# Second weights of the first two experts issued by GpSimd behind the row gathers, with new gather costs in the planner

## Chip, cores and metric

The kernel runs on one core of one Trainium2 chip, in one launch. The metric is the device time of one execution in microseconds. The runs are compared by their medians, and one further execution was profiled.

## What is computed

The reference has three parts in a row, all in float32 (the weights of the middle part come as float64):

- an mLSTM attention over 4 batches, 8 heads, 768 positions and a head dimension of 40, with gates; its output is laid out as 3072 tokens of 320 numbers;
- a feed-forward layer 320 -> 2048 -> 320 with a clipped quadratic activation;
- a mixture of 8 experts. Each token goes to one expert, greedily by the logits of a gate, with at most 384 tokens for an expert:

```python
cap = N // E
for idx in np.argsort(-logits.flatten()):
    tok, e = int(idx) // E, int(idx) % E
    if assigned[tok] >= 0 or counts[e] >= cap: continue
    assigned[tok] = e; counts[e] += 1
for e in range(E):
    h = np.maximum(x[assigned == e] @ w1[e], 0.0)
    out[assigned == e] = h @ w2[e]
```

An expert has 384 tokens, w1 of 320 x 1024 and w2 of 1024 x 320.

## The kernel before, in words

**The stages.** Attention (24 chunks of 128 tokens) runs beside the feed-forward layer (8 groups of 384 tokens, 16 slices of 128 hidden units each) until some 570 us. The result of the feed-forward layer, x2, is written to DRAM (`x2_d`, line 880) 128 rows at a time. Then the experts follow, counted here as the code does, from `ph` = 0 to 7, and called expert 0 to expert 7.

**An expert.** `route(ph)` finds which expert is filled next, and which tokens go to it, by a search over six groups of bits of the logits. Each of its six steps is a short chain VectorE mask `m` (L1039), TensorE count `pc` (L1098), VectorE `ev`, TensorE `ps` (L1112), VectorE `ok`, TensorE `pj` (L1122), VectorE `y`. It yields the expert's number `ei` and, through `slots()`, the indices `idx` of its 384 tokens. `gather(ph, idx)` has GpSimd issue three indirect DMAs (L1253), each of which fetches 128 rows of 1280 bytes out of `x2_d` into `xg`; ScalarE copies a part of the tile (L1257), TensorE transposes it into `pxe` (L639), and `split_x` splits that into a rounded part `xh_e` (ScalarE L641) and a rest `xl_e` (VectorE L645; L647 writes the rest of the last 64 rows into `xh_e`). `weights(ph, ei)` has SyncE read the number of the expert into a register (L1269) and issue the loads: four pieces of w1, each of one DMA of 262 KB and two of 65 KB (L1281, L1284), and four pieces of w2, each of one DMA of 328 KB (L1294, two blocks of 128 rows of 1280 bytes). Each piece is split by ScalarE and VectorE (w1: L1287, L1289; w2: L1296, L1298). The raw pieces have three buffers for each kind, so the fourth piece is loaded when the first is split. `expert()` then runs, for each of eight slices of 128 hidden units, eight matmuls up into `pf` (L788), a ReLU and a split (L1320, L1321), and nine matmuls down into `pe` (L854), two slices behind. At its end the three results are copied into `os` (L1336) and GpSimd scatters them into the output (L1339). `prepare(ph + 1)` (gather and weights of the next expert) is listed inside `expert(ph)` at its ninth turn, and route steps of later experts are put between its matmuls. Until the first gather lands, TensorE is given empty matmuls on a constant (`pdm`, L349).

**What sets the order.** Nothing above is issued where it stands in the source. `add()` makes a step with an engine, an estimated duration `dur`, for a DMA its transfer time `dma`, and a latency `lat`, and with the steps that it needs: by the tiles that it reads and writes, and by the list `after`. `order()` is a list scheduler. It plans all steps by these numbers, and `issue()` then emits them in the planned order of start, so that each engine's instructions have a fixed order. `after` and the costs are known to the planner alone. At run time an engine takes its instructions in that order, and an instruction waits only for the data that it reads and the buffers that it overwrites. For a DMA the planner reckons

```python
if s.dma:
    if e == "S":
        hw = max(hw, end) + 0.45
        dma = max(dma, hw + 0.65) + s.dma
    else:
        dma = max(dma, end + 1.55) + s.dma
    end = dma + 0.9
```

and whatever needs it is ready `lat` (HOP = 0.17 where not given) later. A gather has `dur` 1.05 and `dma` 0.46, so that an undisturbed one lands 1.05 + 1.55 + 0.46 + 0.9 + 0.17 = 4.13 us after its start in the plan, and the third of three 6.23 us after the start of the first.

Of the kernel before, what the change touches and what calls it, by code (L numbers as in the profile page):

```python
# [19 lines left out]
P = 128  # L20
L = 128
TG = 384
HOP = 0.17
# [21 lines left out]
class Plan:  # L45
# [12 lines left out]
    def add(self, eng, dur, fn, r=(), w=(), after=(), dma=0.0, lat=HOP, pre=0, act=1.0, due=None, flat=False):  # L58
        s = Step()
        s.flat = flat  # L60
        s.act, s.due, s.crit, s.mark = act, due, self.crit, self.mark
        s.eng, s.dur, s.lat, s.fn, s.dma = eng, dur, lat, fn, dma
        s.need, s.ready, s.users, s.seq, s.start = 0, 0.0, [], len(self.steps) - pre, None
        s.tiles = []
        deps = set(after)
        for key in r:
            deps.update(self.wr.get(key, ()))
        for key in w:
            deps.update(self.wr.get(key, ()))
            deps.update(self.rd.get(key, ()))  # L70
        for key in r:
            self.rd.setdefault(key, []).append(s)
        for key in w:
            self.wr[key] = [s]
            self.rd[key] = []
        for key in list(r) + list(w):
            t = key[0] if isinstance(key, tuple) else key
            if isinstance(t, Slot) and t not in s.tiles:
                s.tiles.append(t)
                t.left += 1  # L80
        for d in deps:
            d.users.append(s)
            s.need += 1
        self.steps.append(s)
        return s
# [151 lines left out]
def cost_act(n, ap=False, psum=True):  # L237
    return (0.095 if psum else 0.137) + n * 0.00072 + (0.093 if ap else 0.0)


def cost_v(n, fast=False):
    return 0.069 + n * (0.00052 if fast else 0.00104)
# [7 lines left out]
def kernel(  # L250
# [17 lines left out]
    V, A, G, T, S = nc.vector, nc.scalar, nc.gpsimd, nc.tensor, nc.sync  # L268
# [7 lines left out]
    NE = w_gate.shape[1]  # L276
    NC = NTOK // P
# [29 lines left out]
    add = pl.add  # L307

    def at(pool):
        return lambda: pool  # L310
# [10 lines left out]
    def dma(fn, n, r=(), w=(), rate=360.0, after=(), pre=0, dur=0.05, due=None):  # L321
        return add("S", dur, fn, r, w, dma=n / (rate * 1e3), after=after, pre=pre, due=due)
# [43 lines left out]
    x2_d = pl.tile(at(dram), [NTOK, DM], F32, "x2_d", 1)  # L366
# [4 lines left out]
    def c2(t):  # L371
# [6 lines left out]
        r=[gf, gi], w=[gm])  # L378
# [10 lines left out]
        r=[fz, gm], w=[gf])  # L389
# [3 lines left out]
    def t_it():  # L393
# [4 lines left out]
        r=[ps_it], w=[it])  # L398
# [232 lines left out]
    def split_x(x, xh, xl, t, ps, pre=0, due=None):  # L631
        cs = slice(t * P, (t + 1) * P)

        def px():
            return ps()[:, :3 * P].rearrange("p (j l) -> p j l", j=3)

        def t_x():
            for j in range(3):
                T.transpose(px()[:, j, :], x()[:, j * P:(j + 1) * P], ident())  # L639
        add("T", 0.33, t_x, r=[x, identr], w=[ps], due=due)  # L640
        add("A", cost_act(384), lambda: A.activation(xh()[:, :, cs], px(), AF.Copy), r=[ps], w=[(xh, t)])  # L641

        def hf():
            return xh().bitcast(F32)
        add("V", cost_v(256), lambda: V.tensor_tensor(xl()[:, :, cs], px()[:, :2, :], hf()[:, :2, cs], op=OP.subtract),  # L645
            r=[ps, (xh, t)], w=[(xl, t)], pre=pre)
        add("V", cost_v(128), lambda: V.tensor_tensor(xh()[KR:, 2, cs], px()[KR:, 2, :], hf()[KR:, 2, cs], op=OP.subtract),  # L647
            r=[ps], w=[(xh, t)], pre=pre)
# [27 lines left out]
    def piece(name):  # L676
        return pl.tile(at(wpool), [P, 2, 3, 2 * P], F32R, "w1", 8, name)
# [210 lines left out]
    def pd(shape, dtype, name, bufs=1, tag=None):  # L888
        return pl.tile(later("pd"), shape, dtype, tag or name, bufs, name)
# [120 lines left out]
    def psd(tag, name, bufs=1):  # L1010
        return pl.tile(later("psd"), [P, 512], F32, tag, bufs, name)
# [235 lines left out]


    def gather(ph, idx):
        xg = []  # L1250
        for t in range(GC):
            x = pd([P, 3 * P], F32, f"xg{ph}_{t}", 3, "xg")
            add("G", 1.05, lambda t=t, x=x: G.indirect_dma_start(  # L1253
                out=x()[:, :DM], out_offset=None, in_=x2_d(),
                in_offset=bass.IndirectOffsetOnAxis(ap=idx()[:, t:t + 1], axis=0)),
                r=[idx] + [(x2_d, n) for n in range(NC)], w=[x], dma=0.46)
            add("A", cost_act(KR, psum=False), lambda x=x: A.activation(x()[:, DM:], x()[:, 2 * P:DM], AF.Copy), w=[x])  # L1257
            xg.append(x)
        xh = pl.tile(at(p2), [P, 3, TG], F32R, "xh", 2, f"xh_e{ph}")
        xl = pl.tile(at(p2), [P, 2, TG], F32R, "xl", 2, f"xl_e{ph}")  # L1260
        for t in range(GC):
            split_x(xg[t], xh, xl, t, psd("psf", f"pxe{ph}_{t}", 3), 100000)
        return xh, xl

    def weights(ph, ei):
        w1t = [piece(f"w1t{ph}_{i}") for i in range(F2 // (2 * P))]
        w2t = pl.tile(at(wpool), [P, 2, NF2, DM], F32R, "w2", 2, f"w2t{ph}")
        ev = []
        add("S", 1.1, lambda: ev.append(S.value_load(ei()[0:1, 0:1], min_val=0, max_val=NE - 1)), r=[ei], w=[(ei, "reg")])  # L1269
        ek = [(ei, "reg")]  # L1270

        def w1e():
            return w1[bass.ds(ev[0], 1)].rearrange("o d f -> (o d) f")

        def w2e():
            return w2[bass.ds(ev[0], 1)].rearrange("o f d -> (o f) d")
        for s in range(4):
            cs = slice(s * 256, (s + 1) * 256)
            r1 = pd([P, 3, 256], F32, f"r1_{ph}_{s}", 3, "r1")
            hold = late_x[:0] if ph == 0 and s >= 2 else []  # L1280
            dma(lambda cs=cs, r1=r1: S.dma_start(r1()[:, :2, :], w1e()[:2 * P, cs].rearrange("(k p) f -> p k f", p=P)),  # L1281
                262e3, r=ek, w=[(r1, 0)], dur=0.55, after=hold)
            for i in range(2):
                dma(lambda cs=cs, r1=r1, i=i: S.dma_start(r1()[i * KR:(i + 1) * KR, 2, :], w1e()[2 * P:, cs]),  # L1284
                    65e3, r=ek, w=[(r1, 1 + i)], dur=0.55, after=hold)
            rk = [(r1, i) for i in range(3)]
            add("A", cost_act(768, psum=False), lambda s=s, r1=r1: A.activation(w1t[s]()[:, 0], r1(), AF.Copy),  # L1287
                r=rk, w=[(w1t[s], 0)])
            add("V", cost_v(768), lambda s=s, r1=r1: V.tensor_tensor(  # L1289
                w1t[s]()[:, 1], r1(), w1t[s]().bitcast(F32)[:, 0], op=OP.subtract), r=rk + [(w1t[s], 0)], w=[(w1t[s], 1)])  # L1290
        for s in range(4):
            fs = slice(s * 2, (s + 1) * 2)
            r2 = pd([P, 2, DM], F32, f"r2_{ph}_{s}", 3, "r2")
            dma(lambda s=s, r2=r2: S.dma_start(r2(), w2e()[s * 2 * P:(s + 1) * 2 * P, :].rearrange("(k p) d -> p k d", p=P)),  # L1294
                328e3, r=ek, w=[r2], dur=0.55, after=hold)
            add("A", cost_act(640, psum=False), lambda fs=fs, r2=r2: A.activation(w2t()[:, 0, fs, :], r2(), AF.Copy),  # L1296
                r=[r2], w=[(w2t, 0, s)])
            add("V", cost_v(640), lambda fs=fs, r2=r2: V.tensor_tensor(  # L1298
                w2t()[:, 1, fs, :], r2(), w2t().bitcast(F32)[:, 0, fs, :], op=OP.subtract), r=[r2, (w2t, 0, s)], w=[(w2t, 1, s)])
        return w1t, w2t  # L1300
# [47 lines left out]

    def prepare(ph):
        ei, idx = plan[ph]  # L1350
        return (idx, *gather(ph, idx), *weights(ph, ei))

    plan, pend = [], None
    for ph in range(NE):
        pl.crit = ph == 0
        ei, slots = route(ph)
# [12 lines left out]
    if 1:  # L1369
        pdm2 = psd("psf", "pdm2", 3)  # L1370
        add("T", 0.22, filler(pdm2)(2), r=[quart, NEXT], w=[pdm2])
    ready = prepare(0)
    if 1:
        stop = next(st for st in pl.steps if st.eng == "T" and any(x.name == f"pxe0_{0}" for x in st.tiles))
# [44 lines left out]
```

## Time and profile before

| | us |
|---|---|
| runs | 851.94, 852.33, 848.98 (median 851.94) |
| the profiled execution, own time | 848.75 |
| its span in the profile | 847.0 |
| around the span | 1.75 |
| TensorE busy (94% of the span) | 800.3 |
| VectorE busy (74%) | 626.9 |
| ScalarE busy (55%) | 463.9 |
| GpSimd busy (26%) | 221.8 |

The times of the rows below are microseconds from the start of the span. PE is TensorE's matmuls, PEld its weight loads, DVE VectorE, ACT ScalarE, POOL GpSimd, SP SyncE. Instructions that only issue a DMA do not count as busy on SP; the indirect DMAs on POOL do. PEclk is the granted TensorE clock, 1.00 for 2.4 GHz and 0.50 for 1.2 GHz. Where a row groups instructions of one line, it gives the shortest, median and longest in ns; the rows on the tile xg give the time from a gather's issue to its landing. An engine that is idle costs nothing unless what follows on it is late for the end.

### The profile page before, as it was taken

The page shows a single profiled execution, that of the slowest core. Times are in us where ns is not written, and L with a number is a line of the kernel's source. Part 1 is how long each engine was busy: PE and PEld are TensorE (multiplying, and loading weights), DVE is VectorE, ACT ScalarE, POOL GpSimd, SP SyncE. Part 2 cuts the span into 40 slices and gives each one's busy share as a digit, 9 for nine tenths or more (in the row PEclk, how much of TensorE's full clock was granted, in tenths as well). Part 3 has the DMA queues.
Part 4 walks back from the last instruction along what each step waited for, and adds up shares of the span by engine and source line. Part 5 has one row for each costly group of instructions (what it writes and reads, how often), then busy time and mean ns, then how long its engine had stood idle before and what let it go on. Part 6 is the DMA issues. An engine that isn't in the chain of part 4 may idle for free. (4 is left out here: it accounts for less than half of the span.)

```text
span 847.0 us, 15577 instructions
## 1 busy us (share of the span) xinstructions
PE 800.3 (94%) x5493; PEld 748.6 (88%) x5493; DVE 626.9 (74%) x1534; ACT 463.9 (55%) x1002; POOL 221.8 (26%) x315
## 2 busy tenths in 40 slices
PE   8998999999999999999999999997979699999896
PEld 7886889999999999999999998897959598898896
DVE  7888887587877787787887667656768687897561
ACT  4476868666566566566666658803232343543451
POOL 4553555121311310211122143002030321321411
PEclk9999999999999999999999999998969699999998
DMA  9897542231431431532321000005142352452730
GB/s 201 198 224 175 142 136 56 71 70 24 120 77 24 119 73 33 127 72 61 76 49 39 2 1 24 2 13 156 53 131 81 120 152 84 133 161 77 216 100 23
DMA packets 167846, 78.36 MB, mean 93 GB/s; under 512 B 105432, under 2 KB 164056, under 8 KB 167768
## 3 DMA queue, kind: packets, MB, share of 16 engines
q1 hardware_dynamic: 165464, 69.50, 32.0%
q0 software_dynamic: 2304, 7.87, 3.0%
q8 instruction: 43, 0.70, 0.3%
q14 instruction: 35, 0.29, 0.1%
HBM read 69.28 MB, written 8.06 MB: 91 GB/s over the span
## 5 line engine op out<-in xcount | busy, mean ns | idle before, releaser
L788 PE MATMUL ph<-xh,wi 128*128 128x384 f32 x768 | 178.5, 343 | 0.7 <-ACT r L800 0.4
L854 PE MATMUL po<-wo,gh 128*128 128x328 f32 (+1 forms) x690 | 160.3, 316 | 0.2
L788 PEld LDWEIGHTS ph<-xh,wi 128*128 128x128 f32 x768 | 133.3, 189 | 3.3 <-ACT r L800 2.1
L854 PEld LDWEIGHTS po<-wo,gh 128*128 128x128 f32 x690 | 119.1, 190 | 1.0 <-ACT gh L819 1.0
L854 PE MATMUL po<-wo,gl 128*128 128x328 f32 (+1 forms) x345 | 108.9, 316 | 0.9 <-DVE gl L820 0.8
L808 DVE SCALAR_TENSOR_TENSOR r<-r,u 128x384 f32<-128x384 f32 x128 | 78.1, 610 | 33.2 <-ACT u L807 30.9
L788 PE MATMUL pf<-xh_e,w1t 128*128 128x384 f32 x384 | 100.3, 368 | 1.4 <-DVE xh_e L647 1.1
L1320 ACT ACTIVATE hh<-pf 128x384 fp32r<-128x384 f32 x64 | 31.4, 490 | 119.2 <-PE pf L788 92.0
L819 ACT ACTIVATE gh<-r 128x384 fp32r<-128x384 f32 x115 | 60.4, 525 | 65.1 <-DVE r L808 64.9
L798 ACT ACTIVATE u<-ph,half 128x384 f32<-128x384 f32 x128 | 74.1, 579 | 36.6 <-PE ph L788 35.8
L820 DVE TENSOR_TENSOR gl<-r,gh 128x384 fp32r<-128x384 f32 x115 | 72.0, 626 | 25.6 <-ACT gh L819 24.2
L854 PE MATMUL pe<-w2t,hh 128*128 128x320 f32 x384 | 88.4, 316 | 0.0
L788 PE MATMUL ph<-xl,wi 128*128 128x384 f32 x256 | 75.8, 347 | 0.0
L788 PEld LDWEIGHTS pf<-xh_e,w1t 128*128 128x128 f32 x384 | 72.0, 203 | 3.4 <-DVE xh_e L647 1.9
L800 ACT ACTIVATE r<-ph,none 128x384 f32<-128x384 f32 x128 | 74.2, 580 | 0.5 <-DVE st L820 0.5
L807 ACT ACTIVATE u<-u 128x384 f32<-128x384 f32 x112 | 58.9, 526 | 18.6 <-DVE u L806 18.1
L854 PEld LDWEIGHTS po<-wo,gl 128*128 128x128 f32 x345 | 65.2, 189 | 2.2 <-DVE gl L820 2.2
L854 PEld LDWEIGHTS pe<-w2t,hh 128*128 128x128 f32 x384 | 64.3, 189 | 0.2
L854 PE MATMUL pe<-w2t,hl 128*128 128x320 f32 x192 | 59.3, 309 | 0.0
L1321 DVE SCALAR_TENSOR_TENSOR hl<-pf,hh 128x384 fp32r<-128x384 f32 x64 | 35.5, 555 | 30.2 <-ACT hh L1320 29.5
L490 DVE TENSOR_TENSOR_SCAN g<-g,identr 128x1024 f32<-128x1024 f32 x22 | 51.8, 2353 | 1.3 <-DMA g<-fz_d 1.2
L806 DVE TENSOR_SCALAR u<-u 128x384 f32<-128x384 f32 x112 | 43.0, 384 | 11.4 <-ACT u L798 10.5
(220 smaller groups left out, 1631.8 us busy)
## 6 DMA issues: line engine op xcount, KB each, us to landing
g<-fz_d SPq DMA_DIRECT2D x22, 512.0 KB
r<-in_moe_w_dram SPq DMA_DIRECT2D x32, 320.0 KB
r<-in_moe_w_dram SPq DMA_DIRECT2D x32, 256.0 KB
raw<-in_moe_w_out_dram SPq DMA_DIRECT2D x16, 320.0 KB
raw<-in_moe_w_in_dram SPq DMA_DIRECT2D x16, 256.0 KB
r<-in_moe_w_dram SPq DMA_DIRECT2D x64, 64.0 KB
qn<-in_q_dram SPq DMA_DIRECT2D x24, 160.0 KB
kn<-in_k_dram SPq DMA_DIRECT2D x24, 160.0 KB
```

Source lines behind the costliest of these rows:

```text
L490: add("V", 2.25, lambda: V.tensor_tensor_scan(hl(gt()), hl(gt()), hl(identr()), 0.0, op0=OP.mult, op1=OP.add), r=[identr], w=[gt])
L788: T.matmul(ps()[:, :TG], wsrc(m, j), x()[:, j, :], start=(i == 0), stop=(i == len(ops) - 1))
L798: add("A", cost_act(TG, True), lambda: A.activation(u(), ps()[:, :TG], AF.Relu, bias=half(), scale=0.5 / 256), r=[ps, half], w=[u])
L800: add("A", cost_act(TG, True), lambda: A.activation(r(), ps()[:, :TG], AF.Relu, bias=none(), scale=1.0 / 256), r=[ps, none], w=[r])
L806: add("V", cost_v(TG, True), lambda: V.tensor_scalar(u(), u(), 1.0, None, op0=OP.min), w=[u])
L807: add("A", cost_act(TG, psum=False), lambda: A.activation(u(), u(), AF.Square), w=[u])
L808: add("V", cost_v(TG), lambda: V.scalar_tensor_tensor(r(), r(), -0.25, u(), op0=OP.add, op1=OP.add), r=[u], w=[r])
L819: add("A", cost_act(TG, psum=False), lambda: A.activation(hv(), r(), AF.Copy), r=[r], w=[hk])
L820: add("V", cost_v(TG), lambda: V.tensor_tensor(lv(), r(), hv().bitcast(F32), op=OP.subtract), r=[r, hk], w=[lk])
L854: T.matmul(po()[:, :n], a()[:, cs], w(), start=(first and m == 0), stop=(last and m == 2))
L1320: add("A", cost_act(TG), lambda ps=ps, hh=hh: A.activation(hh(), ps()[:, :TG], AF.Relu), r=[ps], w=[hh])
L1321: add("V", cost_v(TG), lambda ps=ps, hh=hh, hl=hl: V.scalar_tensor_tensor(hl(), ps()[:, :TG], 0.0, hh().bitcast(F32), op0=OP.max, op1=OP.s ...
```

## The change

For the experts 0 and 1 (`ph < 2`) the four loads of w2 are issued by GpSimd instead of SyncE. GpSimd reads the number of the expert into a register of its own for that (one more `value_load` for each of the two). In the plan the four loads come after the three gathers of the same expert (`after=sent_x`), with a duration of 1.0 each. For all experts the planner's numbers for a gather change: `dur` from 1.05 to 1.55 (experts 0 and 1) or 1.45 (the others), and `lat` from 0.17 to 1.37 (experts 0 to 2) or 0.37 (the others). No operation on data is added or removed.

```diff
     def gather(ph, idx):
-        xg = []
+        xg, sent_x = [], []
...
-            add("G", 1.05, lambda t=t, x=x: G.indirect_dma_start(
+            sent_x.append(add("G", 1.55 if ph < 2 else 1.45, lambda t=t, x=x: G.indirect_dma_start(
...
-                r=[idx] + [(x2_d, n) for n in range(NC)], w=[x], dma=0.46)
+                r=[idx] + [(x2_d, n) for n in range(NC)], w=[x], dma=0.46, lat=HOP + (1.2 if ph < 3 else 0.2)))
...
-        return xh, xl
-
-    def weights(ph, ei):
+        return xh, xl, sent_x
+
+    def weights(ph, ei, sent_x):
...
+        behind = ph < 2
+        gv = []
+        if behind:
+            add("G", 1.1, lambda: gv.append(G.value_load(ei()[0:1, 0:1], min_val=0, max_val=NE - 1)), r=[ei], w=[(ei, "regg")])
...
         def w2e():
-            return w2[bass.ds(ev[0], 1)].rearrange("o f d -> (o f) d")
+            return w2[bass.ds((gv if behind else ev)[0], 1)].rearrange("o f d -> (o f) d")
...
-            dma(lambda s=s, r2=r2: S.dma_start(r2(), w2e()[s * 2 * P:(s + 1) * 2 * P, :].rearrange("(k p) d -> p k d", p=P)),
-                328e3, r=ek, w=[r2], dur=0.55, after=hold)
+            def f_r2(eng, s=s, r2=r2):
+                eng.dma_start(r2(), w2e()[s * 2 * P:(s + 1) * 2 * P, :].rearrange("(k p) d -> p k d", p=P))
+            if behind:
+                add("G", 1.0, lambda f_r2=f_r2: f_r2(G), r=[(ei, "regg")], w=[r2], dma=328e3 / 360e3, after=sent_x)
+            else:
+                dma(lambda f_r2=f_r2: f_r2(S), 328e3, r=ek, w=[r2], dur=0.55, after=hold)
...
     def prepare(ph):
         ei, idx = plan[ph]
-        return (idx, *gather(ph, idx), *weights(ph, ei))
+        xh, xl, sent_x = gather(ph, idx)
+        return (idx, xh, xl, *weights(ph, ei, sent_x))
```

## Rows read from the trace of the kernel before

**Rows 1.** The page: the chain that ended last, by line.
```profile
PE pf L788 10%; PE pe L854 7%; PE po L854 4%; DMA xg<-x_d,idx 3%; PE pc L1098 2%; PE ph L788 1%; ACT u L807 1%; ACT r L800 1%; ACT u L798 1%; DVE r L808 1%; POOL out_dram L1339 1%; DVE u L806 1%; POOL xg L1253 1%; ACT gh L819 1%; DVE gl L820 1%
```

**Rows 2.** The chain in order of time: start, length, work.
```profile
574.64 2.26 DMA r<-in_moe_w_dram
...
580.26 5.85 DMA xg<-x_d,idx
...
619.15 6.26 DMA xg<-x_d,idx
```

**Rows 3.** Stretches: PE, PEld, DVE, ACT, POOL busy; clock, DMA, GB/s.
```profile
570.00:580.00 10.00, 10.00 (x98) 9.93 (x98) 8.58 (x38) 2.36 (x3) 4.23 (x3) 1.00 0.60 179
580.00:586.00 6.00, 2.69 (x23) 2.06 (x20) 3.06 (x9) 1.07 (x4) 1.73 (x1) 1.00 0.85 269
583.70:586.20 2.50, 0.00 (x0) 0.00 (x0) 0.74 (x2) 0.07 (x1) 0.00 (x0) 1.00 0.73 242
...
588.40:593.40 5.00, 5.00 (x21) 4.69 (x21) 3.55 (x9) 2.05 (x4) 0.00 (x0) 0.50 0.01 2
...
618.80:621.30 2.50, 0.00 (x0) 0.00 (x0) 1.91 (x4) 0.00 (x0) 1.98 (x4) 0.88 0.78 204
...
626.90:634.40 7.50, 7.47 (x32) 5.75 (x33) 4.19 (x15) 1.78 (x4) 0.00 (x0) 0.50 0.01 4
...
730.00:736.00 6.00, 4.78 (x38) 3.65 (x37) 5.10 (x19) 2.82 (x9) 3.14 (x5) 1.00 0.32 108
```

**Rows 4.** SP in order of time: start, length with waits.
```profile
580.37 13.24 SPq L1294 DMA_DIRECT2D r<-in_moe_w_dram  x4
...
618.44 17.78 SPq L1294 DMA_DIRECT2D r<-in_moe_w_dram  x4
```

**Rows 5.** POOL in order of time: gathers of experts 0, 1, 4.
```profile
576.90 1.20 POOL L1253 DMA_INDIRECT xg<-x_d,idx  x1 [4.12 <-DMA r<-in_moe_w_dram]
...
580.26 1.73 POOL L1253 DMA_INDIRECT xg<-x_d,idx  x1 [0.30 <-issue]
608.17 0.18 POOL L1149 TENSOR_TENSOR left<-left,wsel 128x1 f32<-128x1 f32 x1 [26.18 <-DVE wsel L1142]
...
615.58 1.83 POOL L1253 DMA_INDIRECT xg<-x_d,idx  x1 [3.62 <-DVE wm L1073]
...
619.15 1.20 POOL L1253 DMA_INDIRECT xg<-x_d,idx  x1 [0.30 <-PE pj L1122]
...
620.65 1.02 POOL L1339 DMA_INDIRECT out_dram<-os,idx  x1 [0.21 <-issue]
...
724.70 1.48 POOL L1253 DMA_INDIRECT xg<-x_d,idx  x1 [4.51 <-DVE idx L1243]
...
727.97 1.10 POOL L1253 DMA_INDIRECT xg<-x_d,idx  x1 [0.30 <-PE pj L1122]
```

**Rows 6.** Tile xg, three answers: experts 0, 1, 4.
```profile
DMA to landing us min/median/max: 4.6/5.0/5.8
...
DMA to landing us min/median/max: 4.5/5.7/6.3
...
DMA to landing us min/median/max: 3.3/3.6/3.6
```

**Rows 7.** PE in order of time: experts 0 and 1 begin.
```profile
588.36 1.31 PE L788 MATMUL pf<-xh_e,w1t 128*128 128x384 f32 x3
...
595.44 0.54 PE L854 MATMUL pe<-w2t,hh 128*128 128x320 f32 x2
...
626.93 1.69 PE L788 MATMUL pf<-xh_e,w1t 128*128 128x384 f32 x3
...
636.63 0.46 PE L854 MATMUL pe<-w2t,hh 128*128 128x320 f32 x2
```

**Rows 8.** Line 1296, ACT's half of a w2 split.
```profile
L1296 ACT ACTIVATE w2t<-r x8: 727/732/739, 588.0 to 639.4; 128x640 fp32r<-128x640 f32 x8
```

**Rows 9.** Line 1269, SP's read of the expert's number.
```profile
L1269 SPq TENSOR_LOAD <-ei x8: 268/274/479, 569.0 to 776.0; - x8
```

## Prediction

> **What bounds the kernel now.** I read the page's chain first. By line it is mostly TensorE, but 3% of the span is the DMA into xg, the three row gathers of an expert [rows 1]: some 25 us in which TensorE waits for tokens. The chain in order of time shows where: the third gather of expert 0 takes 5.85 us from its issue at 580.26, that of expert 1 takes 6.26 from 619.15 [rows 2]. The view of the tile xg sets that beside other experts: issue to landing is 4.6 to 5.8 us for expert 0, 4.5 to 6.3 for expert 1, but 3.3 to 3.6 for expert 4 [rows 6]. The queues in order of time say what travels beside them. SP begins its w2 loads at 580.37 and 618.44, three at once and a fourth after a wait [rows 4], just ahead of or beside the last gathers [rows 5], and these loads are twice a gather's bytes each (328 KB against 164 KB in the code).
>
> The stretches show the price. From 583.7 to 586.2 TensorE does nothing at full clock; its work up starts at 588.36, and from 588.4 to 593.4 it is busy throughout at 0.50, which is the 1.2 GHz level [rows 3, 7]. In expert 1 it idles from 618.8 to 621.3, where the mean clock of 0.88 says that the lower level began at about 620.7 (2.5 us times 0.88 is 1.9 at 1.00 and 0.6 at 0.50), and it works at 0.50 from 626.9 to 634.4. At the boundary of expert 4, 730 to 736, it is busy 4.78 of 6 us and keeps 1.00 [rows 3]. So a late gather is paid twice: in idle time, and in the slow matmuls after it.
>
> **The change part by part.**
> *Third gather of expert 0.* The question is whether w2 makes it late. By the code's sizes, w1 (1.57 MB), two stores of x2 (0.33) and the gathers (0.49) are 2.39 MB. From 570 to 580 179 GB/s moved 1.79 MB; the 0.6 left take 2.2 us at the 269 GB/s of 580 to 586 [rows 3]. That ends at 582.2, and the gather's issue ends at 581.99 [rows 5]. Without w2 its queue is empty just then. Bounds: 3.3 us as expert 4's fastest [rows 6], and 5.85 as now. I take 3.85, nearest expert 4's: **-2.0 us**, landing at 584.1.
> *The clock of expert 0.* With that landing the empty stretch 583.7 to 586.2 shrinks to 0.4 us, less than the 1.9 after which expert 1's clock fell, and matmuls up begin at some 586.3. Then 5.0 us of full work at 0.50 [rows 3] take 2.5. Bounds 0 and -2.5; I take **-2.5**, as expert 4's boundary with its scattered 1.2 us of idle kept the clock.
> *Third gather of expert 1.* Between 3.3 and 6.26. The scatters of expert 0 still follow it on GpSimd (the first at 620.65 [rows 5]), so I take 4.0: **-2.3 us**, matmuls up at some 624.6 in the old times.
> *The clock of expert 1.* The first gather was issued at 615.58, before any w2 load, and TensorE still has nothing from 618.8 on, so the clock falls as now: **0**. The other end is half of the 7.5 us at 0.50: -3.7.
> *The moved issues.* SP loses eight loads; it waited in them (13.24 and 17.78 us [rows 4]) with nothing urgent behind: 0. GpSimd gains two reads of a number (SP's took 0.27 [rows 9]); it idles 4.12 us before the first gather of expert 0 and 3.62 before that of expert 1 [rows 5], which hides them: 0. It gains eight direct loads, which this trace shows from SP alone. One may cost from next to nothing to 3.7 (twice the longest gather, 1.83, for twice the rows [rows 5]); I take 1.2, as a gather does, and 0.3 between two. In expert 0 GpSimd issues them at 582.3, 583.8 and 585.3, without waiting, since the list `after` binds the plan only. With 3.85 and another 0.6 for 164 KB more at 269 GB/s they land at 586.8, 588.3 and 589.8; a split is 0.73 on ScalarE [rows 8] and, I reckon, as much again on VectorE, so the first piece is ready at 588.3. The first matmul down came 7.1 us after the first up at half clock [rows 7]; now it is wanted no sooner than half of that after 586.3, at 589.9. Hidden by 1.6 us, and 0.9 late at 3.7 an issue, which is this bound's other end. The fourth load waits on GpSimd for its buffer, with nothing queued behind until the small subtraction at 608.17 [rows 5]. In expert 1 the plan holds w2 ready only when the gathers have landed, so the three scatters (1.02 each [rows 5], with 0.3 between) go ahead of it; the loads go out from 624.3 and the first piece is ready at 630.2. The first matmul down came 9.7 after the first up [rows 7], so at 634.3: hidden. Should the loads go ahead instead, the scatters wait 4.5 us and nobody waits for them. Sum of the issues: 0.
> *The planner's new numbers.* They move no work, they reorder it. In the plan the third gather landed 6.23 us after the first was issued; now 8.93 for experts 0 and 1 (two more at 1.55 and 5.83) and 7.63 from expert 3 on. Measured in expert 0: 586.11 - 576.90 = 9.21, and 7.2 if my first term holds; in expert 4: 727.97 + 3.3 - 724.70 = 6.6 [rows 5, 6]. So the old plan was a little early and the new one is 1.0 to 1.7 us late. Bounds for the five boundaries of experts 3 to 7: +1.0 each if steps put behind the landing wait that much longer, -1.2 each if the idle of 730 to 736 [rows 3] goes. I take 0 and keep +5 and -6. For expert 0 the later landing adds empty matmuls ahead of it, which TensorE has idle time for: 0.
>
> Sum: -2.0 - 2.5 - 2.3 = **-6.8 us**. The profiled execution took 848.75 (span 847.0 and 1.75 around it), so 841.95; it is 0.4% below the median of 851.94, and the same step on that median gives **845.1**.
>
> **The rivals.**
> *w2 is not what makes the gathers late (chance 0.26).* The two earlier gathers are late too: 4.6 and 5.0 us in expert 0, 4.5 and 5.7 in expert 1 [rows 6], the first of each issued before any w2 load [rows 4, 5]. Then w1 and the stores do it, and those stay. The price is shared transfer alone: 164 KB take 0.6 us at 269 GB/s, and sharing with one other queue doubles that, so each third gather gains 0.6. TensorE still idles 1.9 us, the clock still falls: -1.2, **850.7**. Against it: the excess over expert 4 is 2.2 and 2.7 us, not 0.6.
> The Trainium skill says so as a rule ("DMA: Bandwidth & Descriptors", section "Anatomy of one DMA"): each DMA engine takes turns between the queue rows it has work for, a packet at a time, so a long load on SP's row should cost a gather on GpSimd's no more than its turn. By that the sum would be -1.2; by the rows, -6.8. The trace speaks for the rows in expert 1, less clearly in expert 0.
> *Expert 1 keeps its clock too (0.14).* If the first gather also lands a microsecond sooner and the new order leaves matmuls down for the gap, the 3.7 us come on top: -10.5, **841.4**. Against it: a piece of w1 and three scatters still travel there.
> *Slower: the orders follow the late plan (0.12).* On each engine the order is fixed, so a copy or transpose that the plan put behind route steps or matmuls waits for these though its rows have landed. Place: TensorE and ScalarE between the landing of xg and the first matmul up. Price: 1.0 us at each of five boundaries, with the gain at the first two eaten by the 1.7 that the plan is late and by a clock that still falls: +5, **857**. It decides from the point where all three xg have landed and the first matmul up comes over 2.5 us later (now 2.2, from 586.11 to 588.36).
>
> **How the numbers follow.** The forecast has 0.48; its own range is 843 to 849 (the third gathers at 5.0 and the clock kept, or at 3.3 and some boundaries better). A measurement here tells 0.5%, 4.3 us, from no change. Faster by more: 0.41 of the forecast's 0.48, all 0.14 of the second rival and 0.02 of the others, 0.57. Within: the rest of the forecast, most of the first rival, a little of the slower one, 0.33. Slower: 0.10. The range 840.5 to 853 takes in all but the slower rival.
>
> **What would show it.** Right: the third gathers land within 4.2 us; no 0.50 stretch in the 10 us after expert 0's first matmul up, which starts near 586; GpSimd shows direct loads straight after the third gather in expert 0. Wrong: gathers still at 5.5 us or more with no w2 beside them (then w1 is the cause); TensorE waiting for a w2 split before its first matmuls down (then a GpSimd load costs over 3 us); boundaries of experts 3 to 7 with over 2 us of idle or a clock of 0.50, where there is none now.

## The result and the profile after

The changed kernel took 841.04 us (median of 4 runs, 838.53 to 841.85) against 850.56 for the kernel before (4 runs, 848.98 to 852.33): a ratio of 0.9893, 95% interval 0.9867 to 0.9919. That is 9.1 us less by the ratio and 9.5 between the medians. The forecast was 6.8 us less. The sign came true, and the time lies in the range 840.5 to 853, but near its lower end, below the forecast's own 843 to 849 and next to the 841.4 of the second rival. The reasons did not come true: as the experiments below show, moving the w2 loads by itself gave nothing, and the new numbers of the planner, which I had counted at 0, gave the gain.

The chain that ended last, on the page of the changed kernel, by engine and by line:

```profile
PE 30%; DVE 6%; ACT 5%; issue 5%; POOL 1%; SPq 0%; DMA 0%; ACTq 0%; POOLq 0%; DVEq 0%
PE pf L788 11%; PE pe L854 9%; PE po L854 3%; PE pc L1098 2%; PE ph L788 1%; ACT u L807 1%; PE pxe L639 1%; ACT r L800 1%; ACT u L798 1%; DVE r L808 1%; DVE u L806 1%; PE pi L1221 1%; ACT gh L819 1%; POOL out_dram L1347 1%; DVE gl L820 1%
```

The 3% of the DMA into xg [rows 1] are gone from it. That looks like the forecast. The queues show whether it is. GpSimd in order of time, in the changed kernel (the last lines of the code have moved down: w2 loads are L1299 now, scatters L1347):

```profile
579.55 1.22 POOL L1253 DMA_INDIRECT xg<-x_d,idx  x1 [4.73 <-DVE di L1042]
...
582.55 1.36 POOL L1253 DMA_INDIRECT xg<-x_d,idx  x1 [0.30 <-issue]
583.90 2.26 POOL L1299 DMA_DIRECT2D r<-in_moe_w_dram  x3
...
605.36 0.18 POOL L1149 TENSOR_TENSOR left<-left,wsel 128x1 f32<-128x1 f32 x1 [9.18 <-DVE wsel L1142]
...
613.18 1.71 POOL L1253 DMA_INDIRECT xg<-x_d,idx  x1 [3.25 <-DVE ys L1127]
...
616.71 1.34 POOL L1253 DMA_INDIRECT xg<-x_d,idx  x1 [0.30 <-issue]
...
622.01 2.26 POOL L1299 DMA_DIRECT2D r<-in_moe_w_dram  x3
```

and ScalarE's copies of the third gathers, which start once these have landed:

```profile
586.92 0.25 ACT L1257 ACTIVATE xg<-xg 128x64 f32<-128x64 f32 x1
...
622.30 0.25 ACT L1257 ACTIVATE xg<-xg 128x64 f32<-128x64 f32 x1
```

The loads stand where the diff put them: right behind the gathers in expert 0, behind gathers and scatters in expert 1. Neither copy shows a wait for its rows, so these starts are upper bounds: the third gather of expert 0 took at most 4.4 us (586.92 - 582.55) against 5.85 [rows 2], that of expert 1 at most 5.6 against 6.26. For expert 0 the trace also has every update of the gather's semaphore, sixteen as before the change; the last, which is the landing, comes 3.4 us after the issue. For expert 1 most of these updates are missing from the trace. Now TensorE at the start of expert 0: search steps (`pc` L1098 to `pj` L1122), transposes (L639), first matmuls up (L788) and down (L854), and the first ones of expert 1:

```profile
579.19 0.82 PE L1098 MATMUL pc<-oh,m 128*128 128x16 bf16 x12
...
581.55 0.16 PE L1122 MATMUL pj<-oka,nw 128*128 128x1 bf16 x1 [0.31 <-issue]
...
582.66 1.02 PE L1098 MATMUL pc<-oh,m 128*128 128x16 bf16 x12
...
585.28 0.17 PE L1122 MATMUL pj<-oka,nw 128*128 128x1 bf16 x1
...
587.37 0.46 PE L1098 MATMUL pc<-oh,m 128*128 128x32 bf16 x6 [0.87 <-DVE m L1039]
587.67 0.88 PE L639 MATMUL pxe<-identr,xg 128*128 128x128 f32 x3
...
588.90 0.16 PE L1122 MATMUL pj<-oka,nw 128*128 128x1 bf16 x1 [0.27 <-DVE ok L1119]
589.13 1.63 PE L788 MATMUL pf<-xh_e,w1t 128*128 128x384 f32 x3
...
596.58 0.45 PE L854 MATMUL pe<-w2t,hh 128*128 128x320 f32 x2
...
624.36 1.31 PE L788 MATMUL pf<-xh_e,w1t 128*128 128x384 f32 x3
...
631.50 0.45 PE L854 MATMUL pe<-w2t,hh 128*128 128x320 f32 x2
```

The matmuls up of expert 0 begin at 589.13, which is later than the 588.36 of before [rows 7], and the down ones at 596.58 instead of 595.44. Part of that comes from before the change: this execution ran the stages up to 517 us some 1.8 us slower. I therefore count from one event that lies ahead of all reordered work, the first matmul of line 830 (517.78 before, 519.59 after). So counted, expert 0's matmuls up begin at 70.6 before and 69.5 after, 1.0 us sooner. The clock was not kept either; stretches of the changed kernel, columns as in [rows 3]:

```profile
586.00:588.00 2.00, 0.96 (x9) 0.78 (x10) 1.84 (x6) 0.75 (x3) 0.17 (x1) 0.91 0.86 310
588.00:590.00 2.00, 1.67 (x10) 1.01 (x8) 1.39 (x7) 1.22 (x2) 0.00 (x0) 0.50 0.35 141
594.00:596.00 2.00, 2.00 (x15) 1.84 (x15) 1.74 (x6) 0.77 (x3) 0.54 (x1) 0.89 0.00 0
...
624.40:629.70 5.30, 5.30 (x28) 4.38 (x28) 3.75 (x12) 3.08 (x5) 0.72 (x1) 0.61 0.46 153
```

What did change is the search. The same part of TensorE's row before:

```profile
580.07 0.16 PE L1122 MATMUL pj<-oka,nw 128*128 128x1 bf16 x1
581.97 0.61 PE L639 MATMUL pxe<-identr,xg 128*128 128x128 f32 x3 [0.96 <-DMA xg<-x_d,idx]
582.64 0.47 PE L1098 MATMUL pc<-oh,m 128*128 128x16 bf16 x6
583.03 0.62 PE L639 MATMUL pxe<-identr,xg 128*128 128x128 f32 x3
586.24 0.58 PE L639 MATMUL pxe<-identr,xg 128*128 128x128 f32 x3 [2.59 <-DMA xg<-x_d,idx]
586.62 0.51 PE L1098 MATMUL pc<-oh,m 128*128 128x16 bf16 x6
588.33 0.16 PE L1122 MATMUL pj<-oka,nw 128*128 128x1 bf16 x1 [0.34 <-DVE ok L1119]
```

Before, the transposes stand between the two halves of one count, so the second half waits at 586.24 for a gather that the search does not need, and one step lasts from 580.07 to 588.33, 8.3 us. After, the step that ends at 585.28 took 3.7 us and the next, to 588.90, 3.6. Three steps of the search for expert 1 are done when expert 0's matmuls begin, instead of two. In the same way the first steps of expert 2's search, around expert 1's gathers, go from 8.0 us to 3.6 (from the same rows at line 1122). A search ends with the small subtraction on GpSimd at line 1149; that for expert 1 at 608.17 [rows 5] and 605.36, those for experts 2 and 3, before:

```profile
647.48 0.23 POOL L1149 TENSOR_TENSOR left<-left,wsel 128x1 f32<-128x1 f32 x1 [23.25 <-DVE wsel L1142]
681.18 0.23 POOL L1149 TENSOR_TENSOR left<-left,wsel 128x1 f32<-128x1 f32 x1 [16.89 <-DVE wsel L1142]
```

and after:

```profile
638.63 0.18 POOL L1149 TENSOR_TENSOR left<-left,wsel 128x1 f32<-128x1 f32 x1 [9.45 <-DVE wsel L1142]
668.86 0.19 POOL L1149 TENSOR_TENSOR left<-left,wsel 128x1 f32<-128x1 f32 x1 [9.03 <-DVE wsel L1142]
```

From the first matmul of line 830 that is 4.6, 10.7 and 14.1 us earlier for experts 1, 2 and 3; the end of the program is 11.9 earlier.

TensorE's waits over the expert stage say the same from the other side (what waited, for what: us in total, times, longest). In front of the transposes, before:

```profile
PE pxe L639 <- DMA xg<-x_d,idx: 11.1, 8, 2.6
```

and after:

```profile
PE pxe L639 <- issue: 1.0, 1, 1.0
PE pxe L639 <- ACT xg L1257: 0.6, 3, 0.2
```

TensorE lost 11.1 us to rows that had not landed, and after the change 1.6 in front of the same transposes. Its waits in the matmuls of the search (lines 1098, 1112 and 1122), counted from the first matmul of line 830, are 10.7 us in both.

### The profile page after: what moved, and what is told of

It reads as the page before. It is cut to its first block, busy times and chain, and to the rows that moved or that the text cites. A ratio compares the mean times of both kernels' runs of the same rounds, so it can differ in the third digit from the quotient of the medians.

```text
span 836.9 us, 15603 instructions
## 1 busy us (share of the span) xinstructions
PE 800.0 (96%) x5493; PEld 748.3 (89%) x5493; DVE 625.8 (75%) x1534; ACT 465.2 (56%) x1002; POOL 228.7 (27%) x323
## 3 DMA queue, kind: packets, MB, share of 16 engines
q1 hardware_dynamic: 163288, 66.88, 31.7%
## 5 line engine op out<-in xcount | busy, mean ns | idle before, releaser
L788 PE MATMUL ph<-xh,wi 128*128 128x384 f32 x768 | 179.0, 343 | 0.7 <-ACT r L800 0.4
L854 PE MATMUL po<-wo,gh 128*128 128x328 f32 (+1 forms) x690 | 159.9, 316 | 0.2
L788 PEld LDWEIGHTS ph<-xh,wi 128*128 128x128 f32 x768 | 133.7, 189 | 3.3 <-ACT r L800 2.0
L854 PEld LDWEIGHTS po<-wo,gh 128*128 128x128 f32 x690 | 118.8, 189 | 1.1 <-ACT gh L819 1.0
L854 PE MATMUL po<-wo,gl 128*128 128x328 f32 (+1 forms) x345 | 108.1, 315 | 0.9 <-DVE gl L820 0.8
L788 PE MATMUL pf<-xh_e,w1t 128*128 128x384 f32 x384 | 99.6, 366 | 0.5 <-issue 0.5
L820 DVE TENSOR_TENSOR gl<-r,gh 128x384 fp32r<-128x384 f32 x115 | 72.1, 627 | 25.6 <-ACT gh L819 24.8
L854 PE MATMUL pe<-w2t,hh 128*128 128x320 f32 x384 | 89.1, 318 | 0.0
L788 PE MATMUL ph<-xl,wi 128*128 128x384 f32 x256 | 75.8, 347 | 0.0
L788 PEld LDWEIGHTS pf<-xh_e,w1t 128*128 128x128 f32 x384 | 70.5, 201 | 3.5 <-issue 2.3
L854 PEld LDWEIGHTS po<-wo,gl 128*128 128x128 f32 x345 | 65.0, 189 | 2.2 <-DVE gl L820 2.2
L854 PEld LDWEIGHTS pe<-w2t,hh 128*128 128x128 f32 x384 | 64.0, 189 | 0.3
L854 PE MATMUL pe<-w2t,hl 128*128 128x320 f32 x192 | 59.3, 309 | 0.0
L806 DVE TENSOR_SCALAR u<-u 128x384 f32<-128x384 f32 x112 | 43.0, 384 | 11.4 <-ACT u L798 10.5
```

The lines of the kernel that those rows point to most:

```text
L788: T.matmul(ps()[:, :TG], wsrc(m, j), x()[:, j, :], start=(i == 0), stop=(i == len(ops) - 1))
L806: add("V", cost_v(TG, True), lambda: V.tensor_scalar(u(), u(), 1.0, None, op0=OP.min), w=[u])
L820: add("V", cost_v(TG), lambda: V.tensor_tensor(lv(), r(), hv().bitcast(F32), op=OP.subtract), r=[r, hk], w=[lk])
L854: T.matmul(po()[:, :n], a()[:, cs], w(), start=(first and m == 0), stop=(last and m == 2))
```

## The experiments

Two theories. **A**, the prediction's: w2 in front delays the gathers, and the move cures that. **B**: the search for the next expert is a serial chain through VectorE and TensorE that paces the experts; a gather that the plan expects too early puts its transposes ahead of search steps in TensorE's fixed order, and the search then waits for tokens that it does not need. The new numbers put more of the search ahead. The runs were made in three groups of four, each on one chip and beside runs of the kernel before there, which took 850.9 us in the first group (the move alone, the numbers alone, the same order, numbers for experts 0 and 1), 848.77 in the second (numbers from expert 2 on, durations, latencies, expert 0 as measured) and 848.49 in the third (late everywhere, later still, expert 2 alone, the move for three). The expectations were written for some 851. A time of the second or third group is therefore read by its distance from its own 848.77 or 848.49, and by the ratio, which is not exactly the quotient of the two medians (up to 0.003 apart).

**The move alone, old numbers.**

```diff
-            sent_x.append(add("G", 1.55 if ph < 2 else 1.45, ...
+            sent_x.append(add("G", 1.05, ...
-                ..., dma=0.46, lat=HOP + (1.2 if ph < 3 else 0.2)))
+                ..., dma=0.46))
```

> The w2 loads of experts 0 and 1 go to GpSimd behind the gathers; the planner's gather numbers stay those of before. Theory A (w2 delays the gathers): the third gathers land within 4.5 us of their issue and the time falls to some 843 to 845. Theory B (the new numbers bring a better order, the move alone little): 849 to 851, about as before.

852.7 us, ratio 1.0032 (1.0005 to 1.006): slightly slower than before, and above the range of B too. Yet the gathers did get faster. GpSimd and ScalarE in this run, expert 0:

```profile
580.03 0.95 POOL L1253 DMA_INDIRECT xg<-x_d,idx  x1 [0.30 <-issue]
580.98 2.25 POOL L1299 DMA_DIRECT2D r<-in_moe_w_dram  x3
```

```profile
583.98 0.39 ACT L1257 ACTIVATE xg<-xg 128x64 f32<-128x64 f32 x2
```

The third lands 3.9 us after its issue, by the last update of its semaphore; in expert 1 it took at most 3.5. What became of it, at expert 1, on TensorE and VectorE:

```profile
617.48 0.16 PE L1122 MATMUL pj<-oka,nw 128*128 128x1 bf16 x1 [0.27 <-DVE ok L1119]
619.21 0.53 PE L1098 MATMUL pc<-oh,m 128*128 128x16 bf16 x6 [1.57 <-issue]
620.52 0.90 PE L639 MATMUL pxe<-identr,xg 128*128 128x128 f32 x3 [0.78 <-DMA xg<-x_d,idx]
621.22 0.51 PE L1098 MATMUL pc<-oh,m 128*128 128x16 bf16 x6
...
624.31 0.16 PE L1122 MATMUL pj<-oka,nw 128*128 128x1 bf16 x1
```

```profile
623.24 0.17 DVE L1106 CAST ev<-pc 128x16 f16<-128x16 f32 x1 [3.52 <-PE pxe L639]
```

The transposes still split a count, the search step still lasts 6.8 us, and VectorE waits 3.5 us for TensorE. The page's chain of this run still has 3% for the DMA into xg, and TensorE still waits in front of the transposes:

```profile
PE pxe L639 <- DMA xg<-x_d,idx: 5.2, 5, 1.9
```

That is 5.9 us less than before. But its waits in the matmuls of the search grew from 10.7 to 15.0 us, so that its idle time stays nearly the same (31.7 against 32.1). The kernel was 7.2 us ahead at expert 2's first matmul down (counted from line 830: 152.1 against 159.3), 2.9 ahead at expert 3's and 0.3 behind at the end. A's mechanism is there; its gain is given back: the wait for tokens turned into waits of the search, and three of the five waits for tokens that are left stand at later boundaries.

**The numbers alone, w2 on SyncE.**

```diff
-        behind = ph < 2
+        behind = False
```

> The new planner numbers for all gathers, w2 loads on SyncE as before. Theory A: the gathers of experts 0 and 1 still take 5 to 6 us, time 847 to 851. Theory B: the route steps stand earlier and most of the gain is there, 841 to 844.

839.72 us, ratio 0.9889 (0.985 to 0.9928): the whole gain of the change. The third gathers are slow as A says: 5.0 us for expert 0, by the last update of its semaphore, and at most 6.1 for expert 1:

```profile
617.44 1.29 POOL L1253 DMA_INDIRECT xg<-x_d,idx  x1 [0.30 <-issue]
```

```profile
623.52 0.26 ACT L1257 ACTIVATE xg<-xg 128x64 f32<-128x64 f32 x1
```

The time is on B's side, 1.3 us below its range, and A is out as the cause of the gain. TensorE's waits in front of the transposes are 0.6 us in all, although the gathers are slow.

**The changed kernel's order, w2 issued by SyncE.** On TensorE, VectorE and ScalarE this kernel has the same instructions in the same order as the changed one.

```diff
-                add("G", 1.0, lambda f_r2=f_r2: f_r2(G), r=[(ei, "regg")], ...
+                add("G", 1.0, lambda f_r2=f_r2: f_r2(S), r=[(ei, "regg"), (ei, "reg")], ...
-            return w2[bass.ds((gv if behind else ev)[0], 1)]...
+            return w2[bass.ds(ev[0], 1)]...
```

> The order of the changed kernel on TensorE, VectorE and ScalarE is kept; only the eight w2 loads are issued by SyncE, which gets to them about 1.5 us (expert 0) and 6 us (expert 1) earlier than GpSimd does. Theory A: the third gathers take 5.5 us or more again and the time is 3 to 6 us above the changed kernel, 844 to 847. Theory B: within 1 us of the changed kernel, 840 to 842.

842.49 us, ratio 0.992 (0.9899 to 0.9942), between the two expectations; its interval overlaps that of the changed kernel. The third gather of expert 0 landed 4.3 us after its issue (3.4 in the changed kernel). That of expert 1 took at most 7.2 us and at least 6.7, where the last update of its semaphore on record lies (at most 5.6 in the changed kernel):

```profile
615.50 1.37 POOL L1253 DMA_INDIRECT xg<-x_d,idx  x1 [0.30 <-issue]
```

```profile
622.67 0.25 ACT L1257 ACTIVATE xg<-xg 128x64 f32<-128x64 f32 x1
```

So with the order held, the move is worth some 1.5 us in the medians and 2.3 by the ratios, no more than these runs can separate from nothing.

**Numbers for some experts only,** with the move. In the first run the new numbers hold for experts 0 and 1, in the second from 2 on, in the third for expert 2 alone:

```diff
-            sent_x.append(add("G", 1.55 if ph < 2 else 1.45, ...
+            sent_x.append(add("G", 1.55 if ph < 2 else 1.05, ...
-                ..., lat=HOP + (1.2 if ph < 3 else 0.2)))
+                ..., lat=HOP + (1.2 if ph < 2 else 0.0)))
```

> As the changed kernel, but the new numbers hold for the gathers of experts 0 and 1 alone; from expert 2 on 1.05 and 0.17 as before. If the 5 us gained between experts 1 and 2 come from expert 2's own gather being planned later, they go: 845 to 847. If they come from the search for the next experts being a step ahead since expert 0, they stay: 840 to 842.

846.88 us, ratio 0.9958 (0.9927 to 0.9989), as the first expectation has it: more than half of the gain is lost without the numbers from expert 2 on.

```diff
+            sent_x.append(add("G", 1.05 if ph < 2 else 1.45, ...
+                ..., lat=HOP + (0.0 if ph < 2 else 1.2 if ph < 3 else 0.2)))
```

> w2 of experts 0 and 1 on GpSimd as in the changed kernel, new numbers from expert 2 on alone, 1.05 and 0.17 for experts 0 and 1. The opposite half of the run with numbers for the first two. Theory B with effects that add (move alone 852.7, numbers of the first two alone 846.9, all 841.0): 846 to 848, and the search for expert 1 ends 3 to 5 us later after the first logit matmul than in the changed kernel (85.8 us after the first one there, 90.4 before). If the search being ahead since expert 0 is needed for the later gain: 849 to 852.

840.58 us against 848.77, ratio 0.9907 (0.9862 to 0.9951): neither expectation, and most of the gain. The search for expert 1 ended at 88.4, between the two. By the search for expert 3 this run had caught up with the one with numbers for experts 0 and 1 (both 153.7), but not with the changed kernel (149.3).

```diff
+            sent_x.append(add("G", 1.45 if ph == 2 else 1.05, ...
+                ..., lat=HOP + (1.2 if ph == 2 else 0.0)))
```

> w2 of experts 0 and 1 on GpSimd, new numbers for the gathers of expert 2 alone. With new numbers from 2 on the time was 840.6, with none 852.7. If the order around expert 2's gathers holds the gain: 840 to 843. If the numbers of experts 3 to 7 are needed to keep what is won earlier (the move alone was 7 us ahead at expert 2's first matmul down and lost it again by the end): 845 to 850.

842.71 us against 848.49, 5.8 us less, ratio 0.9937 (0.9904 to 0.9971). From some 851 that is 845, the low end of the second expectation, though the interval reaches into the first. So the numbers at expert 2 alone, whose loads did not move at all, bring half or more of the gain; that they bring more than those at experts 0 and 1 is not shown, for the two intervals overlap. The parts do not add: each set of numbers gives another order everywhere after it.

**One number at a time, w2 on SyncE.** Durations new and latencies old, then the reverse:

```diff
-                ..., lat=HOP + (1.2 if ph < 3 else 0.2)))
+                ...))
```

> w2 on SyncE, planned gathers of 1.55 and 1.45 but latency 0.17 for all: the third gather of an expert is planned to land 7.7 us after the first issue (6.2 before, 8.9 with both numbers, 9.2 measured before). Theory B, if the planned landing is what counts: about half of the gain, 844 to 847. If only the length on GpSimd counts: 840 to 842.

841.81 us against 848.77, 7.0 us less, ratio 0.9924 (0.9901 to 0.9947).

```diff
-            sent_x.append(add("G", 1.55 if ph < 2 else 1.45, ...
+            sent_x.append(add("G", 1.05, ...
```

> w2 on SyncE, durations 1.05 as before, latencies 1.37 for experts 0 to 2 and 0.37 from 3 on: third landing planned at 7.4 (experts 0 to 2). Theory B, if the planned landing counts: about half of the gain, 844 to 848. If only the latency counts: 840 to 842.

843.8 us against 848.77, 5.0 us less, ratio 0.9947 (0.992 to 0.9973). Either one brings about half of the gain or more, which is what B expected of them; the durations are at the edge of its range. Both push the planned landing of the third gather back.

**Expert 0's landing as measured,** with the move.

```diff
-                ..., lat=HOP + (1.2 if ph < 3 else 0.2)))
+                ..., lat=HOP + (0.0 if ph < 1 else 1.2 if ph < 3 else 0.2)))
```

> As the changed kernel, but latency 0.17 for expert 0, whose gathers land 4.0 to 4.8 us after issue once w2 is behind them (planned 4.6 by that). If a plan that fits the measured landing is best: 838 to 840, below the changed kernel. If what counts is one more search step ahead of expert 0's first matmul up, whatever the landing: that step goes back behind it and the time is 843 to 847.

839.39 us against 848.77, ratio 0.9904 (0.987 to 0.9939): no different from the changed kernel within the intervals, and neither expectation. The profiled execution was the slowest of its five, 843.6. In it the search for expert 1 ended at 88.0 instead of 85.8, and that was not regained: counted from line 830 the program ended 3.1 us after the changed kernel's. So the bulk of the gain does not hang on the one step ahead at expert 0; whether a smaller part does stays open.

**Planned later still, w2 on SyncE.** The late landing for all experts, then 2 us later for the first three:

```diff
+                ..., lat=HOP + 1.2))
```

> w2 on SyncE, the new numbers, with latency 1.37 for every expert instead of 0.37 from expert 3 on, where gathers land in 3.3 to 4.4 us and the plan then says 5.7. Theory B: the search runs no further ahead there, since it already paces the experts, and the tokens wait: 841 to 844, at most 2 us above the run with the numbers alone. If later is simply better: below 839.

834.61 us against 848.49, ratio 0.9862 (0.9813 to 0.9912): the fastest of all, although the plan is now later than the gathers from expert 3 on. My expectation was wrong, and with it the part of B by which the search could not run further ahead there. The interval overlaps the changed kernel's, so that this run beats it is likely and not shown. Its searches for experts 2 and 3 end as early as the changed kernel's or earlier:

```profile
637.85 0.18 POOL L1149 TENSOR_TENSOR left<-left,wsel 128x1 f32<-128x1 f32 x1 [17.38 <-DVE wsel L1142]
666.81 0.24 POOL L1149 TENSOR_TENSOR left<-left,wsel 128x1 f32<-128x1 f32 x1 [9.96 <-DVE wsel L1142]
```

```diff
+                ..., lat=HOP + (3.2 if ph < 3 else 0.2)))
```

> w2 on SyncE, the new numbers, latency 3.37 instead of 1.37 for experts 0 to 2: gathers planned 2 us later than measured. Theory B: one or two further search steps stand ahead of the transposes, which then hold tokens that have landed: 840 to 845, no better than the numbers alone. If the plan has to fit the landing, 845 to 850.

839.18 us against 848.49, ratio 0.9906 (0.9874 to 0.9938), which is no better than the numbers alone, as B expected. Expert 0's matmuls up began at 76.2 (69.5 in the changed kernel), and all of that was regained. The profiled execution was the fastest of its five (834.82) and lost only 4.5 us to the lower clock, against 11.4 in the changed kernel.

**The move for three experts,** with all new numbers.

```diff
-        behind = ph < 2
+        behind = ph < 3
```

> As the changed kernel, with w2 of expert 2 on GpSimd behind its gathers too. Theory A would take another 2 us or so off that expert's wait (its gathers took 4.4 to 5.6 us before): 838 to 840. Theory B: the search sets the pace, 840 to 843.

837.62 us against 848.49, ratio 0.9895 (0.9858 to 0.9932): the same as the changed kernel, so this run does not tell A from B. Moving more buys nothing that shows.

**All runs together.** From each trace, counted in us from the first matmul of line 830: the ends of the searches for experts 1, 3 and 6 (the starts of line 1149's second, fourth and seventh subtraction), and the end of the program. Then TensorE's idle time in between; out of it the waits over 0.15 us in front of the transposes (line 639) and in the matmuls of the search (lines 1098, 1112, 1122); and what its busy time lost at the lower clock (summed over stretches of 2 us).

| run | search 1 | search 3 | search 6 | end | idle | at transposes | in the search | lost at low clock |
|---|---|---|---|---|---|---|---|---|
| before | 90.4 | 163.4 | 256.9 | 329.2 | 32.1 | 11.1 | 10.7 | 13.1 |
| move alone | 89.1 | 158.0 | 254.3 | 329.5 | 31.7 | 5.2 | 15.0 | 13.8 |
| numbers for 0 and 1, move | 86.2 | 153.7 | 251.7 | 326.5 | 26.9 | 3.7 | 9.6 | 15.7 |
| numbers for 2, move | 88.4 | 151.9 | 246.6 | 321.1 | 26.8 | 4.6 | 12.5 | 10.8 |
| numbers from 2 on, move | 88.4 | 153.7 | 247.9 | 321.8 | 25.3 | 2.8 | 12.2 | 13.5 |
| same order, w2 on SP | 85.8 | 151.9 | 248.4 | 321.5 | 25.6 | 2.6 | 11.7 | 11.6 |
| latencies alone | 88.4 | 151.5 | 248.3 | 320.8 | 22.8 | 0.9 | 10.1 | 13.3 |
| durations alone | 86.3 | 152.2 | 246.1 | 319.7 | 23.0 | 1.9 | 11.2 | 13.0 |
| numbers alone | 85.5 | 151.1 | 244.3 | 318.2 | 21.4 | 0.6 | 10.9 | 13.0 |
| the changed kernel | 85.8 | 149.3 | 245.6 | 317.3 | 22.4 | 1.6 | 10.7 | 11.4 |
| expert 0 as measured | 88.0 | 152.2 | 249.0 | 320.5 | 24.0 | 1.5 | 12.5 | 13.4 |
| move for three | 86.2 | 149.3 | 244.8 | 317.7 | 22.0 | 0.8 | 9.9 | 11.8 |
| first three later still | 85.4 | 148.4 | 243.5 | 316.2 | 21.1 | 0.3 | 9.3 | 4.5 |
| late everywhere | 84.2 | 147.8 | 241.0 | 313.2 | 20.7 | 0.7 | 8.8 | 8.9 |

The rest, busy at full clock, is 283.0 to 284.7 in each but one. In "first three later still" it is 290.6; there TensorE was given more of the empty matmuls while it waited for expert 0, 13.1 us of them against 8.5 in the changed kernel.

The end follows the seventh search by 71.5 to 75.2 us in all fourteen, while the ends themselves spread over 16 us. The first matmul up of expert 0, by contrast, lies between 68.5 and 70.6 in all but that one and says nothing of the end.

The two columns of waits tell where the gain sits. The change took 9.7 us of idle time away, and 9.5 of them stood in front of the transposes; 1.7 us are the clock's. The move alone took 5.9 us from the transposes and gave 4.3 back in the search. The new numbers alone left 0.6 us at the transposes and the search's waits as they were. So this much of B is shown: transposes that come late in TensorE's order no longer stop it, and the slow gathers then cost it next to nothing. That the search paces the experts is argued and not shown by itself. TensorE takes all its work in one order, so a stop at the transposes delays the search and the experts' matmuls alike, and no run here holds the search back while it lets the rest go ahead.

## Why the prediction came out right, and where it was wrong

The sign was right and the time lay in the range, by other causes than the ones named. That 6.8 us came near 9.1 is luck: the planner's numbers, which the forecast holds at 0, bring as much without the move, and the move without them brings nothing.

**What the wait costs.** The prediction read the 3% of the chain as "some 25 us in which TensorE waits for tokens". The chain counts a transfer from its issue to its landing. TensorE itself waited 11.1 us for these rows, in eight places, of which expert 2 has 2.0 us and was not looked at.

**Third gather of expert 0 (-2.0).** As a transfer it was right: 3.85 predicted, 3.9 in the run with the move alone, 3.4 in the changed kernel. In the same order with w2 back on SyncE it is 4.3, so the move has 0.9 of the 2.5 us that it fell by in the changed kernel. As time the term failed: counted from line 830 the matmuls up begin 1.0 us sooner after the change, and in the run with the move alone 1.3 sooner at a total that is no shorter. The step that failed is the silent one behind the term, that what TensorE starts earlier at expert 0 arrives at the end.

**The clock of expert 0 (-2.5).** Wrong. The granted clock is at 0.50 from about 587.6 to some 594.4 (the stretches of 2 us above), 6.8 us as before (586.6 to 593.4). In the run with the move alone it fell too, but for 3.4 us (588.5 to 591.9), and that did not show in the time. TensorE worked in pieces there, 0.96 of 2 us from 586 to 588, and the comparison with expert 4's boundary, 4.78 of 6 us, did not carry over.

**Third gather of expert 1 (-2.3).** Of the size, 4.0 predicted, the changed kernel shows only that it was at most 5.6; with the move alone it was at most 3.5. The matmuls up began 4.4 us earlier (104.8 against 109.2, counted from line 830), about as early, 105.3, with the numbers alone and a gather of up to 6.1, and nearly as late as before, 108.5, with the move alone and the fast gather. The gather is not what brought it.

**The clock of expert 1 (0).** It fell, as predicted, but for half as long: 6.8 us (621.8 to 628.6) against 13.7 (620.7 to 634.4), and the work up from 624.4 to 629.7 ran at 0.61 on average against 7.5 us at 0.50 [rows 3].

**The moved issues (0).** Right. A direct load of 328 KB costs GpSimd 0.72 to 0.81 us (three in 2.26), not 1.2, and its matmuls down never waited for w2: ScalarE idled 4.2 us in front of three of the eight w2 pieces of experts 0 and 1, ahead of TensorE's need. The scatters went ahead of the loads in expert 1, as the plan was read.

**The planner's numbers (0, kept between -6 and +5).** This is the mis-sized term. Alone they gave the ratio 0.9889, 9.4 us of 850.9, beyond the bound of -6 that I kept. I priced reordering by the idle time at one boundary (1.2 us at expert 4), five times, gave experts 0 and 1 no term for it beyond empty matmuls, and left expert 2 out, whose new numbers alone gave 5.8 us. And I did not ask what stands behind the transposes in TensorE's order. The rows that would have told it lie in the trace of before: the 11.1 us in front of line 639, and search steps of 8.3 and 8.0 us around the first two experts' gathers, against 2.8 to 3.2 in the search ahead of them.

**The rivals.** "w2 is not what makes the gathers late" said -1.2 for the move and was nearest for the move alone in time, though wrong on the transfer, which did get 1.9 us faster for expert 0 and at least 2.7 for expert 1. The rule of the Trainium skill weighed there ("DMA: Bandwidth & Descriptors"; the page has it in its section "Queues, rings and completion order", not in the one that the prediction names), that engines take turns between queue rows by packets, would have a gather lose only its turn. In the same order the runs show the third gather of expert 0 at 4.3 us with w2 in SP's queue and at 3.4 without, that of expert 1 at 6.7 or more and at 5.6 or less. Both differences are more than the 0.6 I worked out from turns, in one execution each, and the scatters and w1 pieces in flight leave the split open. The second rival, "expert 1 keeps its clock too", comes near by its time, 841.4, and not by its reason: the clock fell there, and the gain is the planner's. The slower rival did not occur: the late plan, far from costing 1 us a boundary, paid.

**The signs.** Of the three signs of being right one came in full, the direct loads straight after the third gather of expert 0. The third gather of expert 0 landed within 4.2 us, that of expert 1 is not known to; and a stretch at 0.50 did follow expert 0's first matmul up. One sign of being wrong came: a stretch at 0.50 from 754.9 to 758.3, at the boundary of expert 5, where there was none.

**Still open.** Which single place gives the gain. Numbers for expert 2 alone, for the first two, or durations alone each give a part, and the parts do not add. How the order itself changed was read only at the boundaries of experts 0 and 1.

## What to carry to other kernels

When a wait looks expensive, ask what stands behind it in the same engine's order before pricing its length: here faster transfers by themselves were worth nothing, for the wait came back in the chain behind them, and putting the waiting instructions later in the fixed order was worth 1.1%. In a kernel whose order comes from a planner, a change of its cost numbers is a change of the whole order and deserves a run of its own; split such a change from any change of real work. A plan that puts a transfer's landing late was better here than one that puts it early; that it is better than one that fits was not shown.

## What the runs showed of the hardware

A direct load issued by GpSimd occupied it for less time than a gather of half the bytes; the changed kernel's line 1299, shortest, median and longest in ns:

```profile
L1299 POOL DMA_DIRECT2D r<-in_moe_w_dram x8: 716/776/805, 583.9 to 628.5; - x8
```

against the gathers of the kernel before, line 1253:

```profile
L1253 POOL DMA_INDIRECT xg<-x_d,idx x24: 942/1223/1832, 576.9 to 791.9; - x24
```

And the clock fell once with no single wait over 1 us just ahead of it: at expert 0 of the changed kernel TensorE was idle for 1.0 of the 2 us from 586 to 588, in pieces, and the lower level came at about 587.6 (0.91 in that stretch).
